# Moving weight and whole-head loads from SyncE's DMA queue to GpSimd's, and converting the weights at other rates

## The chip, the cores and the metric

The kernel runs on one core of one Trainium2 chip. The metric is the device time of the program in microseconds (us). TensorE is called PE (its weight load PEld), VectorE DVE, ScalarE ACT, GpSimd POOL and SyncE SP. A DMA can be issued by SP, whose queue does nothing else, or by POOL, between its own computations.

## The reference

A decayed causal attention over 64 heads (8 batches of 8 heads, 576 positions, 64 wide) is followed by a two-layer MLP with a squared ReLU, all in float32:

```python
scores = scale * np.matmul(q, k.transpose(0, 1, 3, 2))
cum = np.cumsum(np.log(np.clip(f, 0.0001, 1.0)), axis=-1)
decay = cum[:, :, :, None] - cum[:, :, None, :]
scores = np.where(causal, -1000000000.0, scores + decay)
attn = np.exp(scores - np.max(scores, axis=-1, keepdims=True))
attn = attn / (np.sum(attn, axis=-1, keepdims=True) + 1e-09)
x = (attn @ v), heads side by side: 4608 tokens x 512
h = np.maximum(x @ w_in, 0.0)          # 512 x 2048
out = h * h @ w_out                    # 2048 x 512
```

w_in and w_out reach the device as 64-bit floats, and are narrowed there.

## The kernel before, in words

**Attention.** A head is worked in six units, called slots: stretches of keys against queries. Slot n is unit n % 6 of head n // 6, so there are 384 slots, and twelve more run ahead of slot 0. In a slot PE makes the scores (L392 or L399/L402), ACT their exponential (L409), and two slots later PE multiplies by v (L456 or L435 to L437). One head ahead, PE computes the scores once more in another layout (L346) and DVE takes the row maxima from them (L354). Heads 0 to 13 are "whole": PE multiplies them in float32. They need two copies of q and k, a rounded one for the maxima (tile `rk`, `load_rounded`, L287, POOL's queue) and a whole one for the scores (tile `rl`, `load_whole`, L294). Two buffers of each are used in turn. From head 14 on heads are "split" into a rounded high part and a rest, which gives DVE, ACT and POOL further work (`prep`, `split_p`, `split_v`). A store of the cumulated decays to DRAM (L175, `cum_dr`) is read back into spare rows of both copies (L281).

**Dividing.** After every second head, `finish` divides by the row sums in four parts, at fixed numbers of slots behind the head (the table `DIVIDE`, its first row for heads 0 to 7, its second for the others): the sums go to a compact layout by DMA (L481), DVE inverts them and a DMA stores them (L486), a DMA spreads them over the partitions (L489, tile `den`), and POOL multiplies (L492).

**MLP.** Once eight heads are divided, 576 tokens are ready. `split_x` (L509, L510) splits them in chunks of 256, `mlp1` (L522) makes one of 16 blocks of the hidden layer of a chunk, `mlp2` (L545) adds it to the output. `fill` spreads these over the slots up to the next ready slot, on the same PE that does the attention. The first MLP product may stand in slot 60 at the earliest, in head 10.

**Weights.** There are 32 weight blocks of 128 x 512 words of 64 bits (512 KB). `weight_ops` is a generator: `stage` issues a block's load (L194), up to four blocks ahead; then each block takes four steps, in which ACT takes the magnitude (L205), DVE clamps it, shifts it and puts the bits together (L228, L233, L236, L240), ACT makes the rounded part (L210) and POOL the rest (L216). With two steps ahead and two behind there are 132 steps. `cv` in the main loop takes them at `RATES` steps a slot: the first number holds for slots -12 to -7, the second for -3 to -1, the third for 0 to 59, the fourth from slot 60 on.

**What sets the order.** The loop at the end traces the instructions slot by slot; `at(n, half, ...)` hangs work on a slot's first or second half. `in_order` binds PE, ACT, DVE and POOL to that order. SP keeps it only for the instructions ahead of the loop; after that the scheduler sorts SP's queue. The tile framework gives the DMAs of a queue eight semaphores in turn, so a DMA may also wait for the eighth before it.

Of the kernel before, what the change touches and what calls it, by code (L numbers as in the profile page):

```python
# [11 lines left out]
I32 = mybir.dt.int32  # L12
# [22 lines left out]
def decay_attention_relu2_kernel(  # L35
# [18 lines left out]
    nc = tc.nc  # L54

    NH, D, _, S = qk.shape
# [26 lines left out]
    def bank(use):  # L83
# [11 lines left out]
        out=mz[:, MW - P:], in_=mz[:, MW - P:], pattern=[[-1, P]],  # L95
# [6 lines left out]
        out=eye, in_=eye, pattern=[[-1, P]],  # L102
# [83 lines left out]
    def weight_ops():  # L186

        staged, done = {}, {}

        def stage():  # L190
            i = len(staged)
            if i < NW:
                raw = staged[i] = wk.tile([P, 2 * DM], I32, name=f"w{i}", bufs=1)
                nc.sync.dma_start(out=raw, in_=(w_in, w_out)[i % 2][i // 2].bitcast(I32))  # L194

        def words(i):
            w = staged[i].rearrange("p (n t) -> p n t", t=2)
            return w[:, :, 0], w[:, :, 1]

        mags = {}  # L200

        def magnitude(i):
            if i < NW:
                mags[i] = wk.tile([P, DM], F32, name="wmag", bufs=1)
                nc.scalar.activation(out=mags[i], in_=words(i)[1].bitcast(F32), func=AF.Abs)  # L205

        def high_part(i):
            if i >= 0:
                hl = wk.tile([P, 2, DM], F32R, name=f"w{i}", bufs=1)
                nc.scalar.copy(out=hl[:, 0], in_=done[i])  # L210
                done[i] = done[i], hl

        def low_part(i):
            if i >= 0:
                w, hl = done.pop(i)
                nc.gpsimd.tensor_tensor(out=hl[:, 1], in0=w, in1=hl[:, 0].bitcast(F32), op=ALU.subtract)  # L216
                split_w.append(hl)

        stage()
        yield  # L220
        magnitude(0)
        stage()
        yield
        for i in range(NW):
            low, high = words(i)
            mag = mags.pop(i)

            nc.vector.tensor_scalar(mag, mag, MAG_LOW, MAG_HIGH, ALU.max, ALU.min)  # L228
            yield
            w = done[i] = wk.tile([P, DM], F32, name="osb")  # L230
            wi = w.bitcast(I32)

            nc.vector.tensor_scalar(wi, mag.bitcast(I32), 3, 0x3FFFFFFF, ALU.logical_shift_left, ALU.bitwise_and)  # L233
            high_part(i - 1)
            yield
            nc.vector.scalar_tensor_tensor(wi, high, -0x40000000, wi, ALU.bitwise_and, ALU.bitwise_or)  # L236
            low_part(i - 1)
            magnitude(i + 1)
            yield
            nc.vector.scalar_tensor_tensor(wi, low, 29, wi, ALU.logical_shift_right, ALU.bitwise_or)  # L240
            while len(staged) < min(i + 1 + DEPTH, NW):
                stage()
            yield
        high_part(NW - 1)
        yield
        low_part(NW - 1)
        yield
# [17 lines left out]
    NU = len(UNITS)  # L265
# [9 lines left out]
    def load_cum(h, k, r=D):  # L275

        if h == 0:
            for i, c in enumerate(cum):
                nc.sync.dma_start(out=f32(k[r + i:r + i + 1, :S]), in_=c[h:h + 1])
        else:  # L280
            nc.sync.dma_start(out=f32(k[r:r + 2, :S]), in_=cum_dr[h])  # L281
# [9 lines left out]
    def load_whole(h):  # L291

        x = state[h]["whole"] = whole[h % 2]
        nc.sync.dma_start(out=x.raw[:D], in_=qk[h])  # L294
        if cum:
            load_cum(h, x.k, D + 1)

# [293 lines left out]

    RATES = (1, 1.6, 0.8, 2)
    LAG = 2
    NA = H * NU


    DIVIDE = (2, 5, 8, 11), (2, 4, 6, 7)
    MAXIMA = (0, 0.5, 1, 1.5, 2, 2.5), (1.5, 2, 2.5, 3, 3.5, 4)  # L600
    SPLIT = 0, 1, 1, 3
    LOAD = 4
# [9 lines left out]
    def fin(h, part):  # L612

        return (h + 1) * NU - 1 + DIVIDE[h >= H][part]

# [33 lines left out]
    def cv(k):  # L649
        owed[0] += k  # L650
        convert(int(owed[0]))
        owed[0] -= int(owed[0])
# [3 lines left out]
    def at(n, half, do, *args):  # L656
        events.setdefault((n, half), []).append(lambda: do(*args))
# [6 lines left out]
    for h in range(NH):  # L664
        split = h >= NWHOLE
        if split:
            at((h - 2) * NU + LOAD, 0, load, h)
            for part in range(4):
                at((h - 1) * NU + SPLIT[part], 1, prep, h, part)
        else:  # L670
            if h > 1:
                at((h - 3) * NU + 3, 0, load_rounded, h)
                at((h - 2) * NU + 5, 1, load_whole, h)
        at((h - 1) * NU + VLOAD, 1, load_v, h)
        at((h - 1) * NU + VSPLIT, 1, split_v, h)
        for i, x in enumerate(MAXIMA[split]):
            at((h - 1) * NU + int(x), int(2 * x) % 2, max_unit, h, i)
        if not split:
            at((h - 1) * NU + (4 if h else 3), 0, turn_maxima, h)
# [12 lines left out]
    load_f()  # L692
    load_rounded(0)
    load_whole(0)
    constants()
    convert(1)
# [3 lines left out]
    store_cum()  # L700
    load_rounded(1, False)
    load_whole(1)
    load_cum(1, rounded[1].k)
    start = {i.name for i in tc.nc.cur_bb.bb.instructions}
    for n in range(-2 * NU, last_slot + 1):
        live = 0 <= n < len(slots)
        split_last()
        if live:
            h, u = slots[n]
# [11 lines left out]
        for do in events.get((n, 0), ()):  # L721
            do()
        wr = RATES[0] * (n < -NU) if n < -NU // 2 else RATES[1 if n < 0 else 2 if n < ready[0] else 3]
        cv(wr / 2)
# [49 lines left out]
```

## Time and profile before

| | |
|---|---|
| median of 3 runs | 1231.27 us (1229.71 to 1232.37) |
| the profiled execution | 1229.0 us, span 1227.3 us, mean granted PE clock 0.989 |
| busy PE / PEld / DVE / ACT / POOL | 1187.9 / 1047.9 / 781.5 / 710.3 / 376.4 us |
| data moved | 71.88 MB, of which SP's queue 66.26 MB and POOL's 4.13 MB |
| small packets | 88184 of 106376 under 512 B |

Times count from the start of the span. A row of the timeline gives the start, the time it took, the engine, the line and the tiles written and read; a bracket behind it gives the engine's idle time just before and what ended it. SPq is SP's queue. The slices of the page are some 30.7 us long.

### The profile page before, as it was taken

The numbers are of one execution on the slowest core, as the hardware profiler recorded it, in microseconds if no ns is written. First come the engines' busy times: TensorE is split into PE (matmuls) and PEld (weight loads), VectorE is DVE, ScalarE is ACT, GpSimd is POOL, SyncE is SP. The second block draws the span as 40 slices with busy tenths as digits, with TensorE's granted clock in tenths as the row PEclk, the third lists the DMA queues.
The fourth block names the chain that finished last, engine by engine and source line by source line (L and its number), as shares of the span: only waits on it lengthen the run. The fifth ranks groups of instructions, "written<-read, shape, count | busy, mean of one in ns | idle before, by whom it ended". The sixth has DMA issues, their size and how long they took to land.

```text
span 1227.3 us, 23243 instructions
## 1 busy us (share of the span) xinstructions
PE 1187.9 (97%) x7770; PEld 1047.9 (85%) x7770; DVE 781.5 (64%) x2046; ACT 710.3 (58%) x1748; POOL 376.4 (31%) x566
## 2 busy tenths in 40 slices
PE   6997998899999999999999999999999999999998
PEld 3665877788999899999999989998999899999997
DVE  5767778876666767666665666767666667533322
ACT  2774655556666666665656666666666666533232
POOL 3332234533333333332322243333333433200000
PEclk8998999899999999999999999999999999999999
DMA  7777501121221212111111121211111212000000
GB/s 216 209 187 178 185 16 33 25 70 34 48 50 41 59 41 53 37 44 36 49 19 56 26 59 42 58 41 45 38 52 41 59 41 59 11 28 1 18 18 18
DMA packets 106376, 71.88 MB, mean 59 GB/s; under 512 B 88184, under 2 KB 88184, under 8 KB 106256
## 3 DMA queue, kind: packets, MB, share of 16 engines
q1 hardware_dynamic: 105136, 66.26, 21.0%
q0 software_dynamic: 1120, 4.13, 1.4%
q8 instruction: 62, 1.02, 0.4%
q14 instruction: 58, 0.48, 0.1%
HBM read 60.20 MB, written 9.88 MB: 57 GB/s over the span
## 4 chain that ended last, share of the span: by engine, by line
PE 76%; ACT 2%; issue 2%; POOL 1%; DVE 0%; DVEq 0%; POOLq 0%
PE bank L522 30%; PE bank L545 28%; PE bank L435 3%; PE bank L437 3%; PE bank L402 3%; PE bank L436 3%; PE bank L346 3%; PE bank L399 3%; POOL v L333 0%; ACT den L471 0%; ACT p L409 0%; ACT r L530 0%; ACT ph L424 0%; ACT gh L532 0%; POOL p L411 0%
## 5 line engine op out<-in xcount | busy, mean ns | idle before, releaser
L545 PE MATMUL bank<-w,gh 128*128 128x512 f32 x1152 | 412.9, 399 | 0.0
L522 PE MATMUL bank<-xh,w 128*128 128x256 f32 x2304 | 331.5, 287 | 5.5 <-DVE tcol L354 5.5
L522 PEld LDWEIGHTS bank<-xh,w 128*128 128x128 f32 x2304 | 303.5, 191 | 13.2 <-DVE tcol L354 5.9
L425 DVE TENSOR_TENSOR pl<-p,ph 128x320 fp32r<-128x320 f32 (+4 forms) x300 | 186.0, 620 | 196.9 <-ACT ph L424 191.4
L545 PEld LDWEIGHTS bank<-w,gh 128*128 128x128 f32 x1152 | 217.1, 188 | 38.1
L530 ACT ACTIVATE r<-bank 128x256 f32<-128x256 f32 x288 | 110.3, 383 | 220.3 <-PE bank L522 200.3
L545 PE MATMUL bank<-w,gl 128*128 128x512 f32 x576 | 226.8, 394 | 0.1
L531 DVE TENSOR_TENSOR g<-r 128x256 f32<-128x256 f32 x288 | 128.5, 446 | 139.0 <-ACT r L530 138.3
L411 POOL TENSOR_SCALAR_AFFINE_SELECT p<-p 128x128 f32<-128x128 f32 (+1 forms) x250 | 83.6, 334 | 423.6 <-ACT p L409 322.7
L424 ACT CAST ph<-p 128x320 fp32r<-128x320 f32 (+4 forms) x300 | 124.4, 415 | 152.3 <-POOL p L411 110.2
L522 PE MATMUL bank<-xl,w 128*128 128x256 f32 x1152 | 185.6, 284 | 0.0
L522 PEld LDWEIGHTS bank<-xl,w 128*128 128x128 f32 x1152 | 159.3, 192 | 0.0
L533 DVE TENSOR_TENSOR gl<-g,gh 128x256 fp32r<-128x256 f32 x288 | 134.4, 467 | 35.7 <-DVE g L531 0.9
L409 ACT ACTIVATE p<-bank 128x320 f32<-128x320 f32 (+4 forms) x300 | 115.9, 386 | 62.7 <-PE bank L402 51.2
L354 DVE CUSTOM_DVE_ANT_0 bank<-bank,mz 128x256 f32<-128x256 f32 (+4 forms) x320 | 133.5, 432 | 27.4 <-PE bank L346 23.3
L346 PE MATMUL bank<-rk 66*128 66x320 f32 (+4 forms) x384 | 112.5, 318 | 22.0 <-DVE tcol L354 13.4
L532 ACT ACTIVATE gh<-r 128x256 fp32r<-128x256 f32 x288 | 120.4, 418 | 9.2
L545 PEld LDWEIGHTS bank<-w,gl 128*128 128x128 f32 x576 | 109.0, 189 | 14.3 <-DVE gl L533 0.9
L346 PEld LDWEIGHTS bank<-rk 66*128 66x128 f32 (+1 forms) x384 | 68.2, 182 | 40.1 <-DVE tcol L354 16.5
L435 PE MATMUL bank<-pl,vh 128*65 128x320 f32 (+4 forms) x350 | 97.6, 279 | 4.6 <-ACT den L471 4.6
L436 PE MATMUL bank<-ph,v 128*64 128x320 f32 (+4 forms) x350 | 95.2, 272 | 0.0
L437 PE MATMUL bank<-ph,vh 128*65 128x320 f32 (+4 forms) x350 | 93.8, 274 | 0.0
(85 smaller groups left out, 1523.5 us busy)
## 6 DMA issues: line engine op xcount, KB each, us to landing
qkraw<-in_qk SPq DMA_DIRECT2D x50, 288.0 KB
v<-in_v SPq DMA_DIRECT2D x64, 160.0 KB
den<-rdr SPq DMA_DIRECT2D x64, 144.0 KB
out<-osb SPq DMA_DIRECT2D x36, 256.0 KB
w<-in_w_in SPq DMA_DIRECT2D x16, 512.0 KB
w<-in_w_out SPq DMA_DIRECT2D x16, 512.0 KB
rl<-in_qk SPq DMA_DIRECT2D x14, 288.0 KB
rk<-in_qk POOLq DMA_DIRECT2D x14, 288.0 KB, 5.0
```

Of the source, the lines that this page charges most:

```text
L346: nc.tensor.matmul(ps[:m, :n], st["r2"][:D + 2, q0:q0 + m], st["kl0"][:D + 2, k0:k0 + n], start=True, stop=True,)
L354: nc.vector.tensor_tensor_reduce(out=ps[:m, :n], in0=ps[:m, :n], in1=mz[:m, mo:mo + n], op0=ALU.add, op1=ALU.min, scale=-1.0, scalar=init, ...
L424: nc.scalar.copy(out=ph[:kn, :n], in_=p[:kn, :n])
L425: nc.vector.tensor_tensor(out=pl[:kn, :n], in0=p[:kn, :n], in1=ph[:kn, :n].bitcast(F32), op=ALU.subtract,)
L435: nc.tensor.matmul(acc[:D + 1, o], vh, pl[:kn, i], start=first, stop=False)
L436: nc.tensor.matmul(acc[:D, o], vl, ph[:kn, i], start=False, stop=False)
L437: nc.tensor.matmul(acc[:D + 1, o], vh, ph[:kn, i], start=False, stop=last)
L522: nc.tensor.matmul(ph[:, :T], w[:, s, cc], x[:, cc, :], start=(cc == 0 and k == 0), stop=(cc == NCC - 1 and k == 2),)
L531: nc.vector.tensor_tensor(out=g, in0=r, in1=r, op=ALU.mult)
L532: nc.scalar.activation(out=gh, in_=r, func=AF.Square)
L533: nc.vector.tensor_tensor(out=gl, in0=g, in1=gh.bitcast(F32), op=ALU.subtract)
L545: nc.tensor.matmul(po, g[:, ts], w[:, s], start=(fc == 0 and k == 0), stop=(fc == NF - 1 and k == 2),)
```

## The change

Blocks 1 to 31 of the weights, and whole heads 1 to 13, are loaded from POOL's queue; block 0 and head 0 stay on SP's. Whole heads are asked for one slot later, rounded ones too. The conversion goes at 1 instead of 0.8 steps a slot in slots 0 to 59, and at 2.3 instead of 2 behind them. For heads 8 to 63 the multiplication by the inverted sums comes one slot later, and with it the slot from which the block's tokens are ready.

```diff
@@ weight_ops, stage
-                nc.sync.dma_start(out=raw, in_=(w_in, w_out)[i % 2][i // 2].bitcast(I32))
+                (nc.gpsimd if i else nc.sync).dma_start(out=raw, in_=(w_in, w_out)[i % 2][i // 2].bitcast(I32))
@@ load_whole
-        nc.sync.dma_start(out=x.raw[:D], in_=qk[h])
+        (nc.gpsimd if h else nc.sync).dma_start(out=x.raw[:D], in_=qk[h])
@@
-    RATES = (1, 1.6, 0.8, 2)
+    RATES = (1, 1.6, 1, 2.3)
@@
-    DIVIDE = (2, 5, 8, 11), (2, 4, 6, 7)
+    DIVIDE = (2, 5, 8, 11), (2, 4, 6, 8)
@@
-                at((h - 3) * NU + 3, 0, load_rounded, h)
-                at((h - 2) * NU + 5, 1, load_whole, h)
+                at((h - 3) * NU + 4, 0, load_rounded, h)
+                at((h - 1) * NU, 1, load_whole, h)
```

The start, on SP before the change (`w_170` is weight block 1, `rk_80` and `rl` belong to head 1):

```order
L294 DMA rl<-in_qk 64x1152
L281 DMA rl<-cum_dr 2x576
L281 DMA rk_80<-cum_dr 2x576
L194 DMA w_170<-in_w_out 128x1024
L194 DMA w_179<-in_w_in 128x1024
L194 DMA w_181<-in_w_out 128x1024
L194 DMA w_183<-in_w_in 128x1024
L301 DMA v<-in_v 128x5x64
```

The same place in the changed program, on POOL:

```order
L287 DMA rk_80<-in_qk 64x1152
L294 DMA rl<-in_qk 64x1152
L194 DMA w_170<-in_w_out 128x1024
L194 DMA w_179<-in_w_in 128x1024
L194 DMA w_181<-in_w_out 128x1024
L194 DMA w_183<-in_w_in 128x1024
L303 MEMSET v 128x5x2
```

Head 1's whole copy and four weight blocks left SP, where the reads of `cum_dr` stood ahead of the weights, and stand on POOL behind the rounded copy of head 1.

Slot 22, in head 3, where heads 0 and 1 are multiplied by their inverted sums (L492), on POOL before the change (L216's `w_` tiles are split weights):

```order
L216 TENSOR_TENSOR w_568<-osb,w_568 128x512
L492 TENSOR_TENSOR xt_333<-xt_333,den 128x576
L216 TENSOR_TENSOR w_648<-osb,w_648 128x512
L303 MEMSET v 128x5x2
L287 DMA rk_80<-in_qk 64x1152
```

The same place in the changed program:

```order
L216 TENSOR_TENSOR w_580<-osb,w_580 128x512
L492 TENSOR_TENSOR xt_335<-xt_335,den 128x576
L287 DMA rk_79<-in_qk 64x1152
L194 DMA w_617<-in_w_out 128x1024
L294 DMA rl<-in_qk 64x1152
L216 TENSOR_TENSOR w_639<-osb,w_639 128x512
L194 DMA w_680<-in_w_in 128x1024
L303 MEMSET v 128x5x2
```

Behind the multiplication now stand the rounded copy of head 6, a weight block and the whole copy of head 5.

Head 15, on DVE before the change (L313 and L314 round head 16, L425 takes the rest of the exponentials, L531 and L533 belong to the MLP):

```order
L313 CAST rk_79<-qkraw 64x576
L314 CAST rk_79<-qkraw 64x576
L236 SCALAR_TENSOR_TENSOR osb<-w_2133,osb 128x512
L240 SCALAR_TENSOR_TENSOR osb<-w_2133,osb 128x512
L354 ISA bank_2510,tcol<-bank_2510,mz 128x256
L354 ISA tcol 128x1
L228 TENSOR_SCALAR wmag<-wmag 128x512
L425 TENSOR_TENSOR pl<-p,ph 128x320
L531 TENSOR_TENSOR g<-r 128x256
L533 TENSOR_TENSOR gl<-g,gh 128x256
```

The same place in the changed program:

```order
L313 CAST rk_79<-qkraw 64x576
L314 CAST rk_79<-qkraw 64x576
L425 TENSOR_TENSOR pl<-p,ph 128x320 x2
L531 TENSOR_TENSOR g<-r 128x256
L533 TENSOR_TENSOR gl<-g,gh 128x256
L354 ISA bank_2539,tcol<-bank_2539,mz 128x256
L354 ISA tcol 128x1
```

The conversion's instructions (L228, L233, L236, L240) are gone from head 15.

## Prediction

> **What bounds the kernel now.** I read the page's busy times first, then the busy times stage by stage, then the timeline at each place where TensorE (PE) is not full.
>
> ```profile
> span 1227.3 us, 23243 instructions
> PE 1187.9 (97%) x7770; PEld 1047.9 (85%) x7770; DVE 781.5 (64%) x2046; ACT 710.3 (58%) x1748; POOL 376.4 (31%) x566
> PE   6997998899999999999999999999999999999998
> ```
>
> PE is the bound as a whole; its missing tenths stand in the first ten slices (some 300 us). A faster kernel can only come from there. I cut that part at the first exponential (L409) of a head, one of 64, of six slots each; two such cuts and the busy times between cuts follow (bounds, length, then busy time and count of PE, PEld, DVE, ACT, POOL, granted clock, DMA share, GB/s).
>
> ```profile
> 192.17 0.42 ACT L409 ACTIVATE p<-bank 128x320 f32<-128x320 f32 x1
> 240.48 0.42 ACT L409 ACTIVATE p<-bank 128x320 f32<-128x320 f32 x1
> 26.90:104.50 77.60, 73.06 (x413) 47.99 (x411) 56.98 (x175) 56.77 (x140) 25.94 (x35) 1.00 0.78 201
> 104.50:112.00 7.50, 2.00 (x8) 1.30 (x8) 4.03 (x6) 1.89 (x4) 2.66 (x3) 0.76 0.98 212
> 112.00:192.20 80.20, 77.79 (x474) 64.00 (x474) 59.65 (x136) 43.49 (x105) 23.20 (x20) 0.98 0.33 99
> 192.20:240.50 48.30, 41.10 (x246) 36.09 (x245) 41.19 (x87) 27.83 (x68) 24.41 (x27) 0.93 0.13 30
> 240.50:278.70 38.20, 34.54 (x223) 30.95 (x224) 27.03 (x67) 22.60 (x58) 14.56 (x21) 0.96 0.20 57
> 278.70:311.10 32.40, 32.03 (x221) 29.22 (x220) 22.04 (x61) 20.71 (x53) 11.87 (x19) 1.00 0.19 40
> ```
>
> The rows are heads 0 to 9, the gap at the first MLP product, heads 10 to 13, then the pairs 14-15, 16-17 and 18-19. The last three have nearly the same PE work (246, 223, 221 matmuls), yet 14-15 take 48.3 us, 16-17 take 38.2 and 18-19 take 32.4. In 14-15 VectorE (DVE) is busy 41.19 of 48.30 us, the highest anywhere, and PE waits for it:
>
> ```profile
> 200.88 0.64 PE L346 MATMUL bank<-rk 66*128 66x320 f32 x1 [2.36 <-DVE tcol L354]
> 220.94 0.47 PE L346 MATMUL bank<-rk 66*128 66x256 f32 x1 [2.41 <-DVE rk L314]
> ```
>
> So DVE bounds heads 14 and 15, where weight conversion still runs while the split heads already need DVE for their own splits. Two more holes lie earlier: the start and the gap at 104.5.
>
> **Conversion, the part with the largest price.** The conversion is 2 + 4x32 + 2 = 132 steps. Before: 1 + 6x1 + 3x1.6 + 60x0.8 = 59.8 of them by slot 60, and 72.2 at 2 a slot last to slot 96, the end of head 15. Changed: 1 + 6 + 4.8 + 60 = 71.8, and 60.2 at 2.3 end at slot 86, the third slot of head 14. Heads 0 to 9 get 12 steps more (3 weights), heads 10 to 13 get 24x0.3 = 7.2 more (1.8 weights), heads 14-15 lose 19.2 (4.8 weights). The order of the changed program agrees: DVE has no conversion left in head 15. What one weight costs, from the groups by line (busy us, mean ns):
>
> ```profile
> L228 DVE TENSOR_SCALAR wmag<-wmag 128x512 f32<-128x512 f32 x32 | 15.9, 497 | 9.3 <-ACT wmag L205 9.2
> L233 DVE TENSOR_SCALAR osb<-wmag 128x512 int32<-128x512 int32 x32 | 16.9, 529 | 0.7
> L236 DVE SCALAR_TENSOR_TENSOR osb<-w,osb 128x512 int32<-128x512 int32 x32 | 29.4, 919 | 0.3
> L240 DVE SCALAR_TENSOR_TENSOR osb<-w,osb 128x512 int32<-128x512 int32 x32 | 27.0, 843 | 0.4
> L205 ACT ACTIVATE wmag<-w 128x512 f32<-128x512 f32 x32 | 21.4, 668 | 19.9 <-DMA w<-in_w_out 9.8 <-DVE osb L233 9.2 <-DMA w<-in_w_in 0.6
> L210 ACT CAST w<-osb 128x512 fp32r<-128x512 f32 x32 | 19.7, 614 | 1.0 <-DVE osb L240 0.7
> L216 POOL TENSOR_TENSOR w<-osb,w 128x512 fp32r<-128x512 f32 x32 | 43.5, 1359 | 77.6 <-ACT w L210 72.4 <-PE bank L522 4.6 <-DMA w<-in_w_in 0.4
> ```
>
> Per weight DVE pays (15.9 + 16.9 + 29.4 + 27.0)/32 = 2.79 us, ACT 1.28, POOL 1.36. Heads 14-15 so lose 4.8x2.79 = 13.4 us of DVE: 41.2 becomes 27.8, about the 27.03 of heads 16-17, which have no conversion. I take their length: 48.3 - 38.2 = **10.1 us less**. Bounds: 0 (something else holds them) and 13.4.
>
> The price is paid earlier. In heads 0 to 9, 3x2.79 = 8.4 us go onto a DVE busy 57.0 of 77.6 us, beside a PE busy 73.1: 20 us of DVE idle can hide it, but DVE's order is fixed, so each instruction put ahead of a maximum (L354) may hold PE. Bounds 0 and 8.4; I take **2.0 more**, nearer the hidden end because DVE stays at 84%. Heads 10 to 13: 1.8x2.79 = 5.0 us onto 59.7 of 80.2, PE full; bounds 0 and 5.0, taken **1.5 more**. If that cover were gone, both would cost their upper ends.
>
> **The start.** Timeline, last bracket the idle time and its releaser:
>
> ```profile
> 7.64 0.52 POOL L287 DMA_DIRECT2D rk<-in_qk  x1
> 13.92 0.32 SPq L281 DMA_DIRECT2D rl<-cum_dr  x1
> 14.55 0.36 SPq L194 DMA_DIRECT2D w<-in_w_out  x1
> 18.50 0.66 ACT L205 ACTIVATE wmag<-w 128x512 f32<-128x512 f32 x1 [9.82 <-DMA w<-in_w_out]
> 19.19 0.43 DVE L228 TENSOR_SCALAR wmag<-wmag 128x512 f32<-128x512 f32 x1 [8.14 <-ACT wmag L205]
> 19.53 0.42 DVE L354 CUSTOM_DVE_ANT_0 bank<-bank,mz 128x256 f32<-128x256 f32 x1
> 20.07 0.74 PE L346 MATMUL bank<-rk 66*128 66x448 f32 x1 [7.58 <-DVE tcol L354]
> ```
>
> The second weight is queued on SP behind the load of the cumulated decays, which waits for their own store. ACT waits 9.82 us for it, DVE behind ACT, PE behind DVE: 7.58 us. In the changed order POOL issues that weight two places behind the L287 of 7.64, so at about 7.64 + 0.52 + one further load of 0.6 = 8.7 instead of 14.55. It landed 3.95 us after issue; with two loads ahead on its queue I allow up to the 6.6 us that is the slowest landing of POOL's loads (below). ACT then starts at 12.7 to 15.3 instead of 18.5: 3.2 to 5.8 us, taken **4.5 less**. The next things due move along: the first v load stands behind four weights on SP now and behind none then.
>
> **The gap at 104.5.**
>
> ```profile
> 99.37 1.11 SPq L489 DMA_DIRECT2D den<-rdr  x2
> 106.14 1.39 POOL L492 TENSOR_TENSOR xt<-xt,den 128x576 f32<-128x576 f32 x1 [4.05 <-DMA den<-rdr]
> 107.56 1.79 DVE L509 CAST xh<-xt 128x1024 fp32r<-128x1024 f32 x1 [4.74 <-POOL xt L492]
> 111.41 2.08 PE L522 MATMUL bank<-xh,w 128*128 128x256 f32 x8 [5.50 <-DVE tcol L354]
> 256.01 0.59 SPq L489 DMA_DIRECT2D den<-rdr  x1
> 259.40 1.43 POOL L492 TENSOR_TENSOR xt<-xt,den 128x576 f32<-128x576 f32 x1 [2.44 <-DMA den<-rdr]
> 260.86 0.56 DVE L509 CAST xh<-xt 128x768 fp32r<-128x768 f32 x1 [2.02 <-POOL rl L312]
> ```
>
> The denominators took 106.14 - 99.37 = 6.77 us beside weights and heads, and 3.39 us in quiet. Without large transfers ahead on SP's queue I expect a landing between these. Up to 3.4 us of the landing, at most PE's 5.5 us of idle: taken **2.5 less**, bounds 0 and 5.5. At 260.86, DVE waits 2.02 us for the same chain; from head 9 on the multiplication now comes a slot later, so that wait goes: **1.0 less**, bounds 0 and 2.0. Each later block's MLP starts a slot later too; PE is full there, which hides it.
>
> By the Trainium skill, page "DMA: Bandwidth & Descriptors", section "Issuing engines are not separate DMA queues", transfers of all issuers run on the same 16 DMA engines and interleave, and another issuer saves only issue time. By that rule the 2.5 us would be nothing and the median 1220.7; 6.77 against 3.39 us shows that load matters, not which queue.
>
> **POOL's new work.** 31 weights and 13 whole heads are issued there:
>
> ```profile
> L287 POOL DMA_DIRECT2D rk<-in_qk x14: 509/577/702, 2.1 to 120.9; - x14
> DMA to landing us min/median/max: 3.4/5.0/6.6
> 97.86 0.48 SPq L294 DMA_DIRECT2D rl<-in_qk  x1
> 104.47 0.78 PE L392 MATMUL bank<-rl 67*128 67x320 f32 x2 [0.75 <-DMA rl<-cum_dr]
> ```
>
> 44x0.58 = 25.5 us (51 if twice the rows cost twice) fall into heads 0 to 13, where POOL is busy 25.9 of 77.6 and 23.2 of 80.2: hidden, as L216 behind it feeds only the MLP. The whole heads are not hidden alike. A head lasts 77.6/10 = 7.76 us, a slot 1.29; a whole head was issued 104.47 - 97.86 = 6.6 us before its use, and is traced a slot later now: 5.3 us left against a landing of 3.4 to 6.6. For heads 2 to 9: from 0 to 8x1.3 = 10.4 us, taken **1.5 more** since the median lands in 5.0. The rounded heads, a slot later too, keep 8 slots or 10.3 us: nothing.
>
> **Sum.** -10.1 - 4.5 - 2.5 - 1.0 + 2.0 + 1.5 + 1.5 = -13.1 us. The profiled execution took 1229.0 us (span 1227.3 and 1.7 around it), so 1215.9; the median of the runs is 2.3 above it, so **1218.2**.
>
> **Rivals.**
> A, DVE charges in full: heads 0 to 13 are nearly PE bound, but PE there already waits for L354, so all 8.4 + 5.0 us could show. 18.1 - 13.4 - 1.5 = 3.2 less, 1228.1. Against it: 20 us of idle DVE in each stage.
> B, slower: whole heads arrive late. In the changed POOL order L492 stands just ahead of a rounded load, a weight and the whole head of every second head; it waits up to 4.05 us for den above, and the whole head is queued behind a weight of 512 KB. Lateness 4.05 + 6.6 - 5.3 = 5.4 us four times and 1.3 four times is 26.8 in place of 1.5: 1243.5. It decides from 14.6/8 = 1.8 us a head on. Against it: L216 and L492 wait mostly because POOL runs ahead. The skill's same page, section "SWDGE vs HWDGE vs iDMA", speaks for B: POOL's descriptors are written to SBUF, from which DVE can lock it out in some modes; 509 to 702 ns beside a busy DVE show no such lock for 64 rows, and no row shows 128.
> C, heads 14-15 stay as long, held by the splits and POOL's masks: 10.1 less gain, 1228.3.
> That the change does not act can be left out, since the order moves.
>
> **Chances.** Forecast 0.72 (own range 1207 to 1225), A 0.13, B 0.11, C 0.04. About 0.2% (2.5 us) is what a measurement of this kernel tells from no change: 1228.8 to 1233.7 is "same". A and C sit at its edge and go half to faster, half to same; a tenth of B to same. Faster 0.81, same 0.09, slower 0.10. All gains at their upper bounds with no cost, 13.4 + 5.8 + 5.5 + 2.0 = 26.7, give 1204.6; the high end takes in A and C and leaves most of B out: 1205 to 1232.
>
> **What would show it.** Right: PE's wait near 20 us under 4 us and heads starting about 4 us earlier; den landing under 5 us at the gap; heads 14-15 in about 38 us with DVE under 30; heads 0 to 9 within 77 to 82. Wrong: L392 waiting for DMA rl once a head (B), heads 0 to 13 longer by over 8 us (A), or 14-15 still above 45 (C).

## The result, and the profile after

The changed kernel is slower: **1237.17 us** median of 6 runs (1234.32 to 1243.62) against 1230.84 for the kernel before on the same chip (6 runs, 1229.40 to 1232.37); ratio 1.0055, 95% interval 1.0030 to 1.0081. The prediction said 1218.2 and its range ended at 1232. The profiled execution took 1235.13 us. The page of the changed kernel:

```profile
span 1233.3 us, 23214 instructions
PE 1194.7 (97%) x7770; PEld 1048.7 (85%) x7770; DVE 781.3 (63%) x2046; ACT 720.1 (58%) x1748; POOL 403.1 (33%) x610
PE   8897998999999999999999999999999999999998
```

PE is busy 6.8 us more for the same 7770 matmuls, and the span grew by 6.0: the kernel as a whole has no more idle time, but slower matmuls. The stages of the changed kernel, most of them cut at the first exponential of a head (bounds, length, busy time and count of PE, PEld, DVE, ACT, POOL, granted clock, DMA share, GB/s):

```profile
22.40:111.60 89.20, 79.30 (x416) 51.36 (x415) 65.79 (x187) 61.29 (x147) 45.68 (x63) 0.94 0.77 186
111.60:119.00 7.40, 3.34 (x16) 2.97 (x15) 3.54 (x7) 1.84 (x4) 5.08 (x6) 0.63 0.65 155
119.00:197.90 78.90, 75.83 (x464) 61.62 (x464) 70.51 (x144) 46.24 (x108) 32.69 (x36) 0.99 0.36 105
197.90:238.00 40.10, 34.78 (x222) 30.76 (x221) 27.31 (x67) 22.91 (x57) 16.86 (x21) 0.96 0.15 40
238.00:275.75 37.75, 34.27 (x227) 30.17 (x226) 23.73 (x63) 22.03 (x56) 12.13 (x19) 1.00 0.20 50
275.75:1059.72 783.97, 780.10 (x5285) 709.81 (x5284) 520.26 (x1419) 500.60 (x1227) 275.12 (x426) 1.00 0.18 45
1059.72:1233.30 173.58, 169.79 (x1090) 153.46 (x1088) 57.03 (x131) 58.51 (x144) 4.45 (x7) 1.00 0.04 15
```

Of the kernel before, what the prediction did not show: heads 0 to 9 up to the first exponential of head 10, heads 18 to 62, and from head 63 to the end:

```profile
26.89:105.28 78.39, 73.85 (x415) 48.51 (x414) 56.98 (x175) 56.78 (x140) 25.94 (x35) 1.00 0.79 201
278.65:1056.77 778.12, 775.63 (x5282) 707.94 (x5281) 521.72 (x1415) 493.59 (x1227) 273.31 (x427) 1.00 0.19 45
1056.77:1227.30 170.53, 166.94 (x1072) 150.95 (x1070) 57.23 (x131) 57.51 (x142) 3.50 (x7) 1.00 0.04 15
```

| stage | before | after | change | predicted |
|---|---|---|---|---|
| to the first exponential | 26.9 | 22.4 | -4.5 | -4.5 |
| heads 0 to 9 | 77.6 | 89.2 | +11.6 | +2.0 +1.5 |
| gap at the first MLP product | 7.5 | 7.4 | -0.1 | -2.5 |
| heads 10 to 13 | 80.2 | 78.9 | -1.3 | +1.5 |
| heads 14, 15 | 48.3 | 40.1 | -8.2 | -10.1 |
| heads 16, 17 | 38.2 | 37.75 | -0.5 | -1.0 |
| heads 18 to 62 | 778.1 | 784.0 | +5.9 | 0 |
| head 63 to the end | 170.5 | 173.6 | +3.1 | 0 |
| sum | 1227.3 | 1233.3 | +6.0 | -13.1 |

The stages of the kernel before are those of the prediction, and its first cut behind head 9, at 104.5, stands 0.8 us ahead of head 10's first exponential (105.28); in the changed kernel the cut is on it. With the same cut in both, heads 0 to 9 grew by 10.7 us (78.4 to 89.1) and the gap by 0.7.

The start and heads 14-15 gave what was expected or nearly. The loss stands in two places: heads 0 to 9, and everything behind head 18. The tail's 3.1 us are 18 matmuls more (1090 against 1072); heads 14 to 17 have 20 fewer (449 against 469), so this is work that was moved, and about 3 of the 8.7 us gained in heads 14 to 17 are only that (an estimate from the 3.1 us).

**The start** of the changed kernel (start, duration, engine, line; idle time and its releaser in the bracket):

```profile
8.65 0.56 POOL L194 DMA_DIRECT2D w<-in_w_out  x1
14.25 0.36 PE L346 MATMUL bank<-rk 66*128 66x256 f32 x1 [2.66 <-DMA rk<-qkraw]
14.82 0.67 ACT L205 ACTIVATE wmag<-w 128x512 f32<-128x512 f32 x1 [5.36 <-DMA w<-in_w_out]
16.40 0.74 PE L346 MATMUL bank<-rk 66*128 66x448 f32 x1 [0.73 <-DVE tcol L354]
```

The second weight is issued at 8.65 instead of 14.55, and ACT takes it at 14.8 instead of 18.5. PE's wait of 7.58 us is now 0.73.

**The gap** of the changed kernel:

```profile
104.39 1.09 SPq L489 DMA_DIRECT2D den<-rdr  x2
104.73 0.52 POOL L294 DMA_DIRECT2D rl<-in_qk  x1
110.73 0.78 PE L392 MATMUL bank<-rl 67*128 67x320 f32 x2 [0.98 <-ACT pl L409]
111.44 1.40 POOL L492 TENSOR_TENSOR xt<-xt,den 128x576 f32<-128x576 f32 x1 [2.81 <-DMA den<-rdr]
116.22 2.08 PE L522 MATMUL bank<-xh,w 128*128 128x256 f32 x8 [4.06 <-DVE tcol L354]
```

The denominators still took 111.44 - 104.39 = 7.05 us (6.77 before) although neither a weight nor a whole head stands on their queue now: a whole head was issued on POOL 0.3 us behind them. That head itself took 5.9 us and PE waited for it (the 0.98 us ends when it has landed, at 110.64, not at ACT).

**Heads 0 to 9.** Of the 10.7 us, 5.3 are PE's busy time (79.2 against 73.85 for as many matmuls, 415, at a granted clock of 0.94 instead of 1.00), 5.4 idle time. DVE's wait for the row sums, in heads 0 to 9 (us, times, longest), of the kernel before:

```profile
DVE cmp L483 <- DMA cmp<-den: 0.9, 2, 0.5
```

and of the changed one, with PE's waits in the same stretch:

```profile
DVE cmp L483 <- DMA cmp<-den: 8.4, 4, 2.5
...
PE bank L346 <- DVE p L354: 7.2, 10, 1.6
PE bank L346 <- DVE tcol L354: 1.2, 3, 0.7
PE bank L392 <- ACT pl L409: 1.0, 1, 1.0
PE bank L392 <- ACT rl L381: 0.4, 1, 0.4
```

One of the holes, in the timeline of the changed kernel, and two windows of it with the clock (third column from the end):

```profile
74.64 0.54 POOL L194 DMA_DIRECT2D w<-in_w_in  x1
75.17 0.52 POOL L294 DMA_DIRECT2D rl<-in_qk  x1
75.64 1.91 DVE L236 SCALAR_TENSOR_TENSOR osb<-w,osb 128x512 int32<-128x512 int32 x1
75.71 1.28 POOL L216 TENSOR_TENSOR w<-osb,w 128x512 fp32r<-128x512 f32 x1
78.07 0.24 PE L346 MATMUL bank<-rk 66*64 66x64 f32 x1 [1.65 <-DVE p L354]
```

```profile
76.40:79.40 3.00, 1.35 (x9) 0.91 (x9) 2.95 (x9) 0.92 (x3) 2.00 (x4) 0.99 1.07 289
79.40:89.60 10.20, 10.20 (x34) 6.66 (x32) 4.20 (x13) 5.44 (x13) 2.90 (x5) 0.50 0.85 206
```

POOL's L216 had no wait of its own (its row has no bracket): it stood behind the two issues. It then ran beside DVE's L236, which took 1.91 us instead of the usual 0.68 or so, about L216's 1.28 us more; the maximum behind it came late, PE idled 1.65 us, and right behind this hole the clock was at half for 10.2 us. That costs about 5.1 us (half of 10.2, an estimate), nearly all that PE's busy time grew by. Right behind DVE's waits for the sums PE waits for a head's first maximum (`tcol`): 1.2 us in all.

### The profile page after: what moved, and what is told of

Read it like the earlier page. It is cut to its first block, busy times and chain, and to the rows that moved or that the text cites. A ratio compares the mean times of both kernels' runs of the same rounds, so it can differ in the third digit from the quotient of the medians.

```text
span 1233.3 us, 23214 instructions
## 1 busy us (share of the span) xinstructions
PE 1194.7 (97%) x7770; PEld 1048.7 (85%) x7770; DVE 781.3 (63%) x2046; ACT 720.1 (58%) x1748; POOL 403.1 (33%) x610
## 4 chain that ended last, share of the span: by engine, by line
PE 83%; DVE 6%; issue 4%; ACT 2%; DMA 2%; POOL 2%; DVEq 0%; SPq 0%; POOLq 0%; ACTq 0%
PE bank L522 31%; PE bank L545 29%; PE bank L346 4%; PE bank L402 3%; PE bank L399 3%; PE bank L435 3%; PE bank L437 3%; PE bank L436 3%; PE bank L392 2%; PE bank L456 2%; DMA cmp<-den 1%; DVE bank L354 1%; DVE xh L509 1%; DVE osb L236 1%; POOL xt L492 1%
## 5 line engine op out<-in xcount | busy, mean ns | idle before, releaser
L522 PE MATMUL bank<-xh,w 128*128 128x256 f32 x2304 | 327.8, 285 | 4.2 <-DVE tcol L354 4.1
L522 PEld LDWEIGHTS bank<-xh,w 128*128 128x128 f32 x2304 | 301.7, 190 | 10.9 <-DVE tcol L354 4.4
L425 DVE TENSOR_TENSOR pl<-p,ph 128x320 fp32r<-128x320 f32 (+4 forms) x300 | 181.2, 604 | 188.4 <-ACT ph L424 173.6
L411 POOL TENSOR_SCALAR_AFFINE_SELECT p<-p 128x128 f32<-128x128 f32 (+1 forms) x250 | 84.6, 339 | 534.8 <-ACT p L409 398.6
L531 DVE TENSOR_TENSOR g<-r 128x256 f32<-128x256 f32 x288 | 131.9, 458 | 128.6 <-ACT r L530 125.8
L522 PE MATMUL bank<-xl,w 128*128 128x256 f32 x1152 | 184.6, 282 | 0.0
L522 PEld LDWEIGHTS bank<-xl,w 128*128 128x128 f32 x1152 | 158.3, 191 | 0.0
L346 PE MATMUL bank<-rk 66*128 66x320 f32 (+4 forms) x384 | 123.9, 332 | 23.3 <-DVE tcol L354 11.5
L533 DVE TENSOR_TENSOR gl<-g,gh 128x256 fp32r<-128x256 f32 x288 | 124.6, 433 | 34.3 <-DVE g L531 1.0
L346 PEld LDWEIGHTS bank<-rk 66*128 66x128 f32 (+1 forms) x384 | 70.0, 183 | 46.7 <-DVE tcol L354 16.1
L437 PE MATMUL bank<-ph,vh 128*65 128x320 f32 (+4 forms) x350 | 93.6, 273 | 0.0
```

The lines of the kernel that those rows point to most:

```text
L346: nc.tensor.matmul(ps[:m, :n], st["r2"][:D + 2, q0:q0 + m], st["kl0"][:D + 2, k0:k0 + n], start=True, stop=True,)
L425: nc.vector.tensor_tensor(out=pl[:kn, :n], in0=p[:kn, :n], in1=ph[:kn, :n].bitcast(F32), op=ALU.subtract,)
L437: nc.tensor.matmul(acc[:D + 1, o], vh, ph[:kn, i], start=False, stop=last)
L522: nc.tensor.matmul(ph[:, :T], w[:, s, cc], x[:, cc, :], start=(cc == 0 and k == 0), stop=(cc == NCC - 1 and k == 2),)
L531: nc.vector.tensor_tensor(out=g, in0=r, in1=r, op=ALU.mult)
L533: nc.vector.tensor_tensor(out=gl, in0=g, in1=gh.bitcast(F32), op=ALU.subtract)
```

## The experiments

"Heads 0 to 9" below is from the first exponential of head 0 to that of head 10 in the profiled execution (78.4 in the kernel before, 89.1 in the changed one); "late part" is from the first exponential of head 18 to the end (948.7 and 957.6). Medians are in us; the kernel before stood at 1230.6 to 1231.5 beside each.

**One part at a time, from the kernel before.** Only the rates:

```diff
-    RATES = (1, 1.6, 0.8, 2)
+    RATES = (1, 1.6, 1, 2.3)
```

> The kernel before with only RATES (1, 1.6, 1, 2.3); all loads stay on SP's queue. Theory 3 (the wait at L483 comes from the queues): heads 0 to 9 grow by only 1 to 3 us from 78.4, DVE waits under 2 us at L483, heads 14-15 fall by about 8 us from 48.3 as in the changed kernel, so about 1225. Rival 4 (the conversion costs DVE in full there): heads 0 to 9 grow by 8 to 10 us, and the time stays at 1230 to 1232.

1227.11 (1223.40 to 1228.43), ratio 0.9962 (0.9945 to 0.9978). Heads 0 to 9 80.2, and heads 14 to 17:

```profile
26.56:106.78 80.22, 74.35 (x415) 48.50 (x414) 63.34 (x186) 60.73 (x147) 30.85 (x38) 1.00 0.79 204
194.94:235.26 40.32, 37.46 (x239) 33.59 (x239) 28.41 (x70) 23.47 (x60) 16.09 (x23) 0.96 0.20 48
235.26:271.59 36.33, 34.51 (x230) 30.75 (x229) 25.79 (x65) 21.57 (x56) 13.39 (x19) 1.00 0.18 45
```

The same 469 matmuls in heads 14 to 17 take 76.7 us instead of 86.5: 9.8 less, where 10.1 were foreseen (the 1.0 for head 17 hung on the later multiplication). The price in heads 0 to 9 is 1.8, where 2.0 was foreseen. This part of the change does what it was predicted to do.

The rates and weight blocks 1 to 4 on POOL (`(nc.gpsimd if 0 < i < 5 else nc.sync)` in `stage`):

> The kernel before with the new RATES and only the weight blocks 1 to 4 on POOL's queue. The start alone: PE's wait for the first maximum falls from 7.6 us to 3 or 4, head 0 starts 4 us earlier (22.5 instead of 26.6), heads 0 to 9 stay at about 80 us; 1223 against 1227.1 with the new RATES alone. If the start's gain is given back at a later wait, 1227.

1223.20 (1221.85 to 1226.20), ratio 0.9940 (0.9921 to 0.9960): 3.9 under the rates alone, and the first exponential at 22.2 instead of 26.6. Four loads give nearly the whole gain of the start.

The rates and weight blocks 1 to 31 on POOL:

```diff
-                nc.sync.dma_start(out=raw, ...)
+                (nc.gpsimd if i else nc.sync).dma_start(out=raw, ...)
```

> The kernel before with the new RATES and the weight blocks 1 to 31 on POOL's queue; whole heads stay on SP's, slots and DIVIDE as before. To be set against the run with the new RATES alone (1227.1 us, heads 0 to 9 in 80.2 us, start of head 0 at 26.6 us). Theory 5 (the weights on a second queue share the DMA engines packet by packet with v's 640 small packets, so that v lands late and the sums behind it too): cmp lands 3 to 5 us after its issue instead of 1.5, DVE waits 5 to 8 us at L483, heads 0 to 9 take 86 to 90 us; head 0 starts 4 us earlier; 1229 to 1231. Rival 6 (the whole heads, asked for a slot later, are what costs): heads 0 to 9 stay at 80 to 82 us and the time is about 1223.

**1221.66** (1217.79 to 1224.49, 4 runs), ratio 0.9922 (0.9896 to 0.9948), the fastest of all by its median: it beats both kernels, though its interval overlaps that of the run with four blocks. It is the changed kernel without the move of the whole heads, without the later slots and without the later multiplication. So the loss lies in those three. Heads 0 to 9 take 80.7 us, as rival 6 had it.

The rates and the whole heads on POOL at the changed slots, the weights left on SP:

> The kernel before with the new RATES and whole heads 1 to 13 on POOL's queue at the changed slots; the weights stay on SP's. Theory 5: little contention beside v, DVE waits under 3 us at L483, heads 0 to 9 take 80 to 83 us, 1226 to 1229. Rival 6: heads 0 to 9 take 86 to 90 us, with PE waiting at L392 for DMA rl, and 1232 to 1235.

1233.92 (1227.04 to 1236.22), ratio 1.0014 (0.9994 to 1.0034): 6.8 above the rates alone. Heads 0 to 9 take 88.8.

**One part undone.** The changed kernel with the multiplication at its old slot, `DIVIDE = (2, 5, 8, 11), (2, 4, 6, 7)`:

> The changed kernel with the second row of DIVIDE back at (2, 4, 6, 7), so that the multiplication and the ready slot of the later blocks stand where they stood before. Theory 1 (the later ready slot shifts the MLP against the heads, which costs PE some 0.08 us a head and 0.7 us a block, and puts 1.3 more halves into the tail): from the first exponential of head 18 to the end it returns from 957.6 us (1233.3 - 275.7) to about 948.7 (1227.3 - 278.7), so 9 us less than the changed kernel, 1228 against 1237, and a little below the kernel before. Rival 2 (the slower late part comes from the queues or the conversion, or from that execution): head 18 to the end stays at 957 and the time at 1236 to 1237.

1230.88 (1226.35 to 1237.55), ratio 0.9994 (0.9972 to 1.0017): 6.3 less than the changed kernel. The late part is 951.8 instead of 957.6. Heads 0 to 9 stay long (96.7 in the profiled execution, the slowest of its ten). In it PE's longest wait at a whole head's scores reads as "issue":

```profile
70.73 0.52 POOL L294 DMA_DIRECT2D rl<-in_qk  x1
78.48 0.78 PE L392 MATMUL bank<-rl 67*128 67x320 f32 x2 [2.66 <-issue]
DMA to landing us min/median/max: 4.9/5.8/7.7
```

The last row is that of L294 on POOL: the slowest landing of ten, 7.7 us, fits the head issued at 70.73, which PE waits for until 78.48. So whole heads on POOL do arrive late at times; three such waits in this profile are 1.33, 2.66 and 1.70 us. Behind the first two the clock fell to half, at 59.0 and 79.5. It did so behind a late whole head in other profiles too: at 43.4 with the whole heads alone (a wait of 1.39 us), at 84.6 with the later inversion (3.05) and at 80.7 with the queue alone (2.20; the last two runs follow).

The kernel before with that multiplication's slot only, `(2, 4, 6, 8)`:

> The kernel before with only the second row of DIVIDE at (2, 4, 6, 8). Theory 1: head 18 to the end grows from 948.7 to about 957 us; heads 0 to 15 unchanged; 1238 to 1240 against 1231. Rival 2: no change, 1231. The prediction on record would have it 1 us faster.

1243.45 (1239.04 to 1247.67), ratio 1.0099 (1.0067 to 1.0130): 11.9 above the kernel before beside it (1231.53). The late part is 958.1, and heads 14-15 52.1. The prediction on record had counted this edit as 1.0 us of gain.

**Whole heads: the queue or the slot?** The kernel of 1221.7 with whole heads on POOL at the old slots:

> The run with the weights on POOL's queue (1221.7 us, heads 0 to 9 in 80.7 us, DVE's wait at L483 4.0 us), and whole heads 1 to 13 on POOL's queue too, at the slots of the kernel before. Theory 9 (the queue costs: a whole head then shares the engines with the sums instead of standing ahead of them): heads 0 to 9 take 86 to 90 us, DVE waits over 7 us at L483, 1228 to 1231. Rival 10 (the later slot costs, on whichever queue, since it puts the whole head into flight beside the sums): heads 0 to 9 stay at 80 to 82 us and the time at 1221 to 1223.

1224.05 (1222.65 to 1230.04), ratio 0.9958 (0.9938 to 0.9978).

The same kernel with the later slots of both copies, whole heads on SP:

> The run with the weights on POOL's queue, whole heads on SP's, but asked for at the changed slots (both the rounded and the whole ones a slot later). Theory 9: heads 0 to 9 stay at 80 to 82 us, 1221 to 1223. Rival 10: heads 0 to 9 take 86 to 90 us, 1228 to 1231, DVE's wait at L483 over 7 us.

1223.76 (1219.73 to 1227.81), ratio 0.9944 (0.9924 to 0.9964). Either alone costs some 2 us by medians, which the intervals do not tell from nothing; both together cost 1230.88 - 1221.66 = 9.2. Heads 0 to 9 are 86.8 with the queue, 81.1 with the slot, 96.7 with both: theory 9 had the first two right, but not the time of the run with the queue. That the two make more than their sum agrees with a lateness that has a threshold (over the first 125 us the whole heads landed in 4.7 us in the median with the queue alone and in 5.8 with both, and the slot takes 1.3 us of slack); but the profiles of heads 0 to 9 differ from one execution to the next, as the last runs below show, so how the 9.2 us split between queue and slot stays open. How much of it is clock can be told: the mean granted clock of all runs is 0.991 without the move (4 runs, mean 1221.4 us) and 0.986 with it (10 runs, 1231.7). The span times the clock that is missing grows from 10.7 to 17.8 us, so by this estimate some 7 of the 10.3 us between the means are slower clock.

**The sums that DVE waits for.** The changed kernel with the inversion (L483) one slot later, `DIVIDE = (2, 6, 8, 11), (2, 4, 6, 7)`:

> The changed kernel with DIVIDE (2, 6, 8, 11), (2, 4, 6, 7): the inversion (L483, L484) of heads 0 to 7 one slot later, so that DVE meets it after the sums have landed; the second row as before. Theory 3 (heads 0 to 9 are 10.7 us longer because DVE waits 8.4 us in four places at L483 for the sums, DMA cmp): DVE's wait at L483 falls from 8.4 to under 2 us, heads 0 to 9 from 89.1 to 81 to 84 us, the time 5 to 8 us below the run with only the second row undone, about 1221. Rival 4 (the three weights more in that stage cost DVE in full and the wait only fills time that was lost anyway): heads 0 to 9 stay at 87 to 89 us, and the time at that of the run with the second row undone.

1230.61 (1228.94 to 1239.54), ratio 1.0007 (0.9986 to 1.0027), the same as without the later inversion (1230.88). DVE's wait for the sums did not go, 9.4 us in four waits, so this run tests nothing of what the wait costs. The rows of DVE say why: a head's six maxima stand in the first three slots, so a slot later only one 0.4 us conversion instruction more stands ahead of L483.

The kernel with the old multiplication slot, and the v loads of heads 0 to 13 on POOL as well:

> The changed kernel with the second row of DIVIDE undone (1230.9 us, DVE's wait at L483 8.1 us) and the v loads of heads 0 to 13 on POOL's queue too, so that SP's queue holds small transfers alone. Theory 5 (the sums land late because they stand behind v on SP's queue): cmp lands 1.5 to 2.5 us after its issue, DVE's wait at L483 falls under 2 us, heads 0 to 9 shrink from 89 to 97 to about 82 to 84 us, and the time to about 1224, unless POOL's issue of 640 packets is itself slow. Rival 7 (the sums land late because any transfer on SP's queue waits for the large ones, packet by packet): cmp still lands after 3 us or more, and the time stays at 1230 or above.

1231.80 (1229.88 to 1234.70), ratio 1.0008 (0.9996 to 1.0019): no gain. The sums, now with no v load ahead on SP's queue, still landed 3.8 us after their issue at the second head of a pair (1.8 in the kernel before, 4.0 in the changed one, 3.1 with the weights alone on POOL). So it is not v ahead on the queue. What does go with it is what moves on the other queue meanwhile (landing is counted here to the last packet). The same place in the changed kernel, and then in that of 1221.7:

```profile
40.99 0.52 SPq L481 DMA_DIRECT2D cmp<-den  x1
45.82 0.17 DVE L483 TENSOR_SCALAR cmp<-cmp 128x9 f32<-128x9 f32 x1 [2.37 <-DMA cmp<-den]
48.80 0.47 PE L346 MATMUL bank<-rk 66*128 66x448 f32 x1 [0.68 <-DVE tcol L354]
```

```profile
40.14 0.48 SPq L481 DMA_DIRECT2D cmp<-den  x1
43.70 0.17 DVE L483 TENSOR_SCALAR cmp<-cmp 128x9 f32<-128x9 f32 x1 [1.10 <-DMA cmp<-den]
```

Up to some 1.1 us of it is hidden; at 2.37 the next head's first maximum is late and PE waits. Both have a weight and a rounded head on POOL at that moment; the changed one had issued a whole head there 4 us earlier.

That the sums come late is shown; that this makes the loss is not, and a later run speaks against it. With the weights alone on POOL and `ready` one slot later (below), heads 0 to 9 took 81.6 us, with next to no half clock, although DVE waited nearly as long for the sums:

```profile
DVE cmp L483 <- DMA cmp<-den: 6.9, 4, 2.1
```

**The gap.** The kernel of 1221.7 with the first block's ready slot two later (`+ 2 + 2 * (b == 0)` in `ready`):

> The run with the weights on POOL's queue, and the ready slot of block 0 alone two slots later, so that DVE meets the split of the first tokens (L509) after POOL's multiplication and PE has two more slots of attention ahead of the first MLP product. If the gap there (PE idle 4.2 us, then the clock at half for 6.8 us) is only a matter of that order, PE's wait at the first L522 falls under 1.5 us and the time by 3 to 6 us, to 1216 to 1219. If the MLP then starts too late against its pace or shifts against the heads, the time stays at 1222 or grows.

1228.53 (1223.52 to 1230.77), ratio 0.9977 (0.9963 to 0.9992): slower by 6.9 than without. (The edit also moves the change of `RATES` from slot 60 to 62.) PE's wait at the first L522 did fall, from 4.20 to 0.52 us, but a hole of 3.15 us then stands ahead of it, and heads 14 to 17 take 81.5 us instead of 76.6. The rest of the loss of this execution stands in heads 0 to 9, 88.4 us with 17.5 at half clock, where nothing was edited; how much of the 6.9 belongs to the gap is not told apart.

**The loss behind head 18.** The later multiplication moves two things: the multiplication itself, and with it `ready`, the slot from which the MLP's halves are spread. The kernel before with `ready` of blocks 1 to 7 one later, the multiplication left (`+ 2 + (b > 0)`):

> The kernel before with the ready slots of blocks 1 to 7 one later, and the multiplication where it was (DIVIDE as before). Theory 1 (the loss behind head 18 comes from the MLP's shift by a slot against the heads): head 18 to the end takes about 957 us instead of 948.7 and the time is 1238 to 1243, as with DIVIDE (2, 4, 6, 8) in the kernel before (1243.5). Rival 8 (it comes from the later multiplication, through POOL's order): head 18 to the end stays at 949 to 950 us, 1231.

1232.49 (1230.45 to 1234.23), ratio 1.0014 (1.0002 to 1.0026): 1.9 more. The late part is 955.8, 7.1 more, of which 3.5 are the tail's 18 moved matmuls (1090 against 1072).

Then the same on the kernel of 1221.7. The multiplication alone (`DIVIDE` with 8, `ready` with `+ 2 - (b > 0)`; the first chunk of each later block is then split ahead of the last pair's multiplication, so that division is left out for it):

> Kernel before with the new rates and the weight blocks on POOL's queue (1221.7 us), and the multiplication of heads 8 to 63 a slot later, but the slot from which a block's tokens count as ready left where it was. Theory O (the loss behind head 18 comes from where the MLP's pieces fall between the products of the attention): the MLP stays where it was, so 1221 to 1224 us, a steady head at 16.22 us, 779 to 781 us from head 18 to head 63, 1072 matmuls behind the first exponential of head 63. Rival M (the late multiplication itself holds up the blocks): 1225 to 1229 us, with the loss at the block boundaries.

1228.06 (1222.93 to 1234.23), ratio 0.9982 (0.9957 to 1.0007).

`ready` alone:

> The same kernel of 1221.7 us, with only the ready slot of blocks 1 to 7 one later and the multiplication left. Theory O: 1225 to 1228 us; a steady head at 16.31 us, 783 to 785 us from head 18 to head 63 with as many matmuls (5282 to 5285), PE busy 4 to 5 us longer there, 18 matmuls more behind head 63. Rival M: within 2 us of 1221.7.

1224.70 (1219.67 to 1231.53), ratio 0.9953 (0.9930 to 0.9975).

Both:

> The same kernel with both, that is the whole change without the whole heads' move and without the later slots of their loads. Theory O: as with the ready slot alone, 1225 to 1228 us. Rival M: as with the multiplication alone, 1225 to 1229, and clearly above the ready slot alone. If both cost: 1229 to 1233.

1231.28 (1227.68 to 1234.51), ratio 0.9992 (0.9970 to 1.0014). Heads 18 to 62 in these four kernels, first the one of 1221.7, then the multiplication alone, `ready` alone, both:

```profile
265.82:1045.09 779.27, 776.23 (x5282) 707.96 (x5281) 521.65 (x1415) 493.66 (x1228) 274.13 (x427) 1.00 0.19 45
```

```profile
278.49:1061.56 783.07, 777.48 (x5282) 708.58 (x5281) 510.79 (x1416) 489.16 (x1228) 271.26 (x426) 1.00 0.19 45
```

```profile
262.53:1043.52 780.99, 777.65 (x5285) 710.36 (x5284) 519.85 (x1419) 500.70 (x1227) 273.47 (x426) 1.00 0.19 45
```

```profile
273.51:1057.59 784.08, 780.11 (x5285) 709.89 (x5284) 520.40 (x1419) 500.42 (x1227) 274.97 (x426) 1.00 0.19 45
```

Neither theory holds alone; what was foreseen if both cost, 1229 to 1233, came. By medians the multiplication costs 6.4, `ready` 3.0, both 9.6; in heads 18 to 62 they cost 3.8, 1.7 and 4.8. They cost in different ways: the multiplication leaves the order of matmuls alone and adds mostly idle time (3.0 us become 5.6): all 5280 matmuls that start in this stretch stand in the same order. `ready` changes the order. Its mark is the steady head, 16.31 instead of 16.22 us without any wait in it, and this group (count, busy, mean ns) of the stretch from 296 to 1059 us, in the kernel before and in the changed one:

```profile
L346 PE MATMUL bank<-rk 66*128 66x320 f32 (+4 forms) x264 | 70.2, 288 | 0.1
```

```profile
L346 PE MATMUL bank<-rk 66*128 66x320 f32 (+4 forms) x264 | 79.8, 302 | 1.0 <-DVE rk L314 1.0
```

The 264 products of L346 keep PE 9.6 us longer because the MLP's halves now stand between other products. Of this, 3.7 us are longer single products (264 times 14 ns); the rest comes from products that follow each other and overlap in the records of the first kernel (76.1 us one by one, 70.2 together) and do not in the other. The kernels with `ready` alone show the same means, 303 ns, and the one with the multiplication alone does not, 288. Other lines gain part of it back.

From head 18 to the end the four kernels take 950.2, 954.0, 955.5 and 957.9 us: 3.8, 5.2 and 7.7 more, of which 3.5 and 2.8 with the later `ready` are the tail's 18 moved matmuls. With `ready` alone heads 14 to 17 have 21 matmuls fewer and give 2.4 us back; with both they have as many fewer and give back 0.3. So most of the 9.6 us of both lies behind head 18.

The profiled executions of the multiplication alone and of both are longer in heads 0 to 9 too, though nothing that they change stands there. Heads 0 to 9 of five kernels that differ only behind them (the one of 1221.7, `ready` alone, both, the gap's run, the multiplication alone) took 80.7, 81.6, 87.9, 88.4 and 93.6 us, with 0, 0, 14, 17.5 and 24 us at half clock: the lengths differ by about half of that. So such a difference between two single profiles says nothing of an edit. Over all runs with both the mean granted clock is 0.991, as in the kernel of 1221.7, so their 9.6 us are not clock; with the multiplication alone it is 0.988, and by the same estimate as above some 4 of the 7.3 us between the means are.

## Why the prediction was wrong, point by point

**Right.** Heads 14 and 15, 10.1 us less because DVE loses 13.4 us: DVE fell from 41.19 to 27.31 us (foreseen 27.8), and the length of heads 14 to 17 by 9.8 us with the rates alone. The start, 4.5 less: 4.5, and four loads on POOL suffice. The conversion in heads 0 to 9, 2.0 more: 1.8 with the rates alone. The sign that was named for rival A, heads 0 to 13 longer by over 8 us, did appear in the changed kernel, but its cause did not: the conversion alone costs those 1.8 us.

Two terms of the sum carry 15 of the 19.0 us by which the forecast missed: the later multiplication (7.3) and the move of the whole heads (7.7). The gap's 2.5 come next.

**Wrong: the later multiplication, counted as 1.0 us of gain in head 17, with "Each later block's MLP starts a slot later too; PE is full there, which hides it."** PE was full, and that did not hide it. A PE that is full pays for an order of products that runs slower, and `ready` changed the order in each head: 0.09 us where the heads are steady. The later multiplication adds idle time of its own. Together they cost 6.3 us in the changed kernel, 9.6 on the kernel of 1221.7 and 11.9 on the one before.

**Wrong: the whole heads on POOL, a slot later, 1.5 more.** By medians the move cost 9.2 (1221.66 to 1230.88). The term was reckoned from the length of PE's waits for a late whole head alone. Such waits occur, under the names "issue" and ACT, as rival B said, but they are 1.0 us in heads 0 to 9 of the changed kernel and 5.7 in that with the multiplication at its old slot, and not 26.8. What the sum had no price for is the half clock that begins behind holes of PE: some 7 us by the estimate above. Two more things were left out, whose own cost no run shows. The small transfers on SP's queue are not spared by loads on another queue: the sums landed in 4.0 instead of 1.8 us, and DVE waited 8.4 us for them in four places. And POOL's 44 issues were taken as hidden, "as L216 behind it feeds only the MLP"; but L216 moved by them holds up DVE's instructions, as in the hole at 78.07.

**Wrong: the gap, 2.5 less, with "den landing under 5 us".** It landed in 7.05 us and the gap stayed. The rule of the Trainium skill that the prediction set beside this term, page "DMA: Bandwidth & Descriptors", section "Issuing engines are not separate DMA queues", was the better guide here: by it this term was nothing, and the slow sums agree with it. The gain of the start does not contradict it, since it comes from the order of issue (a weight ahead of a load that waits), not from a second path.

**Wrong, small: head 17, 1.0 less.** DVE's wait for POOL went from 2.02 only to 1.79 us, and the split now meets another POOL instruction. Head 17 of the changed kernel:

```profile
260.54 1.43 POOL L492 TENSOR_TENSOR xt<-xt,den 128x576 f32<-128x576 f32 x1
261.93 1.41 POOL L321 TENSOR_TENSOR rl<-qkraw,rk 64x576 fp32r<-64x576 f32 x1
262.00 1.76 DVE L509 CAST xh<-xt 128x768 fp32r<-128x768 f32 x1 [1.79 <-POOL xt L492]
265.20 0.41 PE L346 MATMUL bank<-rk 66*128 66x320 f32 x1 [2.48 <-DVE tcol L354]
```

L509 took 0.56 us in the kernel before; beside L321 it takes 1.76, and PE waits 2.48 us for the next maximum, 2.17 before.

With the rates and the weights alone on POOL, the terms of the prediction that were kept (-10.1, -4.5, +2.0, +1.5) make -11.1, and the kernel came out 9.2 us faster. The two edits that were costed at 1.5 more and 1.0 less turned this into +6.3: in medians 1230.8, 1227.1 with the rates, 1221.7 with the weights, 1230.9 with the whole heads, 1237.2 with the later multiplication.

## What to carry to other kernels

A step that is moved on an engine with no idle time still has a price: what changes is the order in which that engine works, so cost it by the mean duration of the same instruction next to other neighbours, or measure it alone, before writing "hidden". A small transfer on a quiet queue is not protected from large ones on another; look at what is in flight when someone waits for it. Where four edits go together, the two that carry the gain may be paying for the two that were thought free. And look at the granted clock before reading two profiles against each other: here the same ten heads took 80.7 to 93.6 us, mostly by the time at half clock.

## What the hardware showed that was not expected

- A transfer of 64 rows of 36 bytes took 1.8 us to land with no load on POOL's queue and 4.0 beside weights and heads there (second head of a pair, mean of four, to the last packet).
- A DVE instruction of the conversion that begins while POOL's L216 runs waits until that is over. In the kernel before and in the changed one L236 and L240 then ended some 0.55 us behind L216, and L228 and L233 0.28 to 0.34 (but for one L233, at 147.47 in the changed kernel). So L236 takes up to 1.77 us where 0.68 is usual and L233 up to 1.5 instead of 0.42. One that begins just ahead of L216 was held in some places (L236, 1.9 to 2.3 us) and in others kept its time, and L216 mostly took longer, up to 1.7 us instead of 1.28. Summed over the conversion's instructions beside L216 in heads 0 to 9, what they take above the usual makes 7.2 us in the kernel before and 10.0 in the changed one. The Trainium skill, page "GPSIMD Engine Reference", section "Key points", says that GpSimd shares its SBUF interfaces with VectorE and contends with instructions that have two SBUF inputs or run in a 2-port performance mode. The rows of L236 and L240, which have two SBUF inputs, agree; whether L228, L233 and L509 run in such a mode no run here shows.
- Half clock in heads 0 to 9 mostly began behind a hole of PE, of 1.23 us (the kernel before with the later multiplication) to 3.05 us (inversion later), but not behind every one: 1.52 us at 60.22 in the changed kernel and 1.61 at 95.09 with the rates alone passed without, and with the multiplication alone a stretch began at 67.2 with no hole over 0.9 us ahead. A stretch that began there lasted 3.4 to 13.7 us, so a hole can cost several times its length, and executions of one such kernel differ by up to 12 us.
